# Weight preparation in the opening of a windowed-attention and Mish feed-forward kernel: the engine that scales, rounds and subtracts, and the place of one weight operation

## The chip, the cores and the metric

One Trainium2 chip, of which the kernel uses one core. The metric is the time on the device in microseconds, lower is better. A core has five engines that run their own instruction queues in order and wait for each other on semaphores: TensorE (PE in the rows, its weight loads PEld), VectorE (DVE), ScalarE (ACT), GpSimd (POOL) and SyncE (SP), which here only issues transfers.

## The reference

```
scores = q @ k.T / sqrt(64)              # 8 sequences x 8 heads, 576 positions, head size 64
mask   = (rel >= 0) & (rel < 64)         # each query sees itself and the 63 keys before it
attn   = softmax(scores, masked)
x      = (attn @ v)                      # put together to 4608 tokens x 512
h      = x @ w_in                        # 512 -> 2048
g      = h * tanh(softplus(h))           # Mish
out    = g @ w_out                       # 2048 -> 512
```

The two weight matrices come as 64-bit floating-point numbers, all else in 32 bits.

## The kernel before

**Products in three parts.** Each feed-forward product is made of a high and a low part in a 32-bit format that TensorE reads in one pass: high times high, high times low, low times high. The high part is a rounded copy (xh, gh, wh), the low part the difference to it (xl, gl, wl). So each value needs a rounding copy and a subtraction.

**Weight pieces.** w_in and w_out are loaded in pieces of 128 x 512 numbers of 64 bits into a buffer st (three of them in turn), and every piece is made into 32-bit numbers there. st is seen as pairs of 32-bit words, lo and hi; an operation on one of them steps over every second word. For a piece the generator `stream` (lines 480 to 493) does in turn: the scale of hi by a power of two (`w_scale`), a shift of lo and a clamp of hi (`w_ready`, two TENSOR_SCALAR rows on st), two joins of hi into lo (`w_joined`, two SCALAR_TENSOR_TENSOR rows on st), the round to wh (`w_round`, a CAST row wi<-st or wo_h<-st) and the subtraction to wl (`w_rest`, a TENSOR_TENSOR row wi<-st,wi or wo_l<-st,wo_h), after which the next load into the freed buffer is issued on SP (`w_load`). The next piece's scale is called between the joins of the piece ahead of it. After two pieces of w_in (tile wi) they alternate between w_out (tiles wo_h, wo_l) and w_in. Shift, clamp, joins and subtraction are VectorE's; who scales and rounds is looked up in the table `by`, which the opening changes as it goes. `some(n)` (line 684) takes n steps of the generator; a step is one of shift, clamp, first join, second join, subtraction.

**The opening.** The first 768 tokens (two chunks of 384) are brought through attention in eight units, a unit being one chunk and one pair of heads. A hand-written software pipeline (lines 743 to 809) works on several units at once: iteration u makes the values of unit u - 2 (TensorE, o_ps), the softmax of unit u (VectorE's masks with the row maximum, pr<-s_ps,masks; ScalarE's exponentials; then sm by GpSimd, a reciprocal by VectorE, and pr<-pr,sm by GpSimd), the transposes of unit u - 1 (t_ps on TensorE) and their copies pT (half by ScalarE, half by VectorE), and the parts of x of unit u - 2: xh by ScalarE (`rest_high`), xl by VectorE (`rest_low`). Between these it takes as many weight steps as the table OPS says.

```
    OPS = (0,2,2,2,3,2,2,2,4,3)
```

Every engine runs these instructions in the order of the code, so the place of a line is its place in the engine's queue. In iteration u the order on VectorE is masks of unit u + 1, xl of unit u - 2, the OPS[u] weight steps, the copy pT of unit u - 1, the reciprocal of unit u. Iterations 7 to 9 are written out; the first feed-forward products (h_ps) begin in iteration 6, part by part.

In the first iteration the table `by` is set to ScalarE for the scale and GpSimd for the round; in iteration 7 the round goes back to ScalarE (line 784). After the loop the steps of both chunks follow, a feed-forward slice of 128 at a time, first h_ps and Mish, two slices later the output products (acc), with five weight steps to each; there VectorE, ScalarE and TensorE work on as in the opening, GpSimd builds thinner masks (`thin_masks`, six copies) and is otherwise free until about 104 us.

Of the kernel before, what the change touches and what calls it, by code (L numbers as in the profile page):

```python
# [11 lines left out]
F32 = mybir.dt.float32  # L12
# [4 lines left out]
ALU = mybir.AluOpType  # L17
# [3 lines left out]
OFFSET = 2.0 ** -112  # L21
# [9 lines left out]
def tile_window_attn_mish_ffn(  # L31
# [57 lines left out]
    vec, act, pool, load = (InTurn(e) for e in (nc.vector, nc.scalar, nc.gpsimd, nc.sync))  # L89
# [54 lines left out]
    def acc_bank(t, name):  # L144
        return ps_acc.tile([P, CH], F32, name=name, tag=f"acc{t}")

    def h_bank(name, width=CH):
        return ps_h.tile([P, width], F32, name=name, tag="h_ps")
# [5 lines left out]
    def at_bank(name, width=CH):  # L154
        at_last[0] = next(at_turn)
        return ps_at.tile([P, width], F32, name=name, tag=f"at{at_last[0]}")

    def at_set(n, name):
        return ps_at.tile([P, DO], F32, name=name, tag=f"at{n}")
# [211 lines left out]
    def function(h_ps):  # L371
        shape = list(h_ps.shape)
        t = mp.tile(shape, F32, name="t", tag="t", bufs=TS)
        gh = mp.tile(shape, F32R, name="gh", bufs=GHS)
        gl = mp.tile(shape, F32R, name="gl", bufs=GLS)

        with tc.high_priority(offset=SOON):
            act.activation(t, h_ps, AF.Mish)
            act.activation(gh, h_ps, AF.Mish)
            if held[0]:  # L380
                residues.append((gl, t, gh))
            else:
                pool.tensor_tensor(gl, t, gh.bitcast(F32), ALU.subtract)
        return gh, gl
# [3 lines left out]
    def residue():  # L388
        while residues:
            gl, t, gh = residues.pop(0)  # L390
            vec.tensor_tensor(gl, t, gh.bitcast(F32), ALU.subtract)
# [48 lines left out]
    def w_load():  # L440
        if pieces:
            fn, f = pieces.pop(0)
            loaded.append(fn(f))
# [25 lines left out]

    def w_rest(piece):  # L470
        lo, hi, wh, wl = piece
        vec.tensor_tensor(wl, lo.bitcast(F32), wh.bitcast(F32), ALU.subtract)
        w_load()
        yield

# [4 lines left out]
    def stream():  # L480

        for piece in w_scale(by["scale"]):
            yield from w_ready(piece)
            while piece:
                joined = w_joined(piece)
                yield next(joined)
                ahead = next(w_scale(by["scale"]), None)
                yield next(joined)
                w_round()
                if ahead:  # L490
                    yield from w_ready(ahead)
                yield from w_rest(piece)
                piece = ahead

    def scaled_by(engine):
        return lambda out, in_: engine.tensor_scalar(out, in_, OFFSET, None, ALU.mult)

    rounding = []
    by = {"scale": scaled_by(vec), "round": act.copy}

    slow = []

# [116 lines left out]
    def products_of(u):  # L619
        a, p = units[u]  # L620
        if u == 0:
            banks = [b for t in range(NM) for b in ([at_bank("s_ps"), at_bank("s_ps")], [acc_bank(0, "s_ps"), acc_bank(1, "s_ps")],
                                                     [h_bank("s_ps"), h_bank("s_ps")])[t]]
        elif u % 2 == 0:
            banks = [acc_bank(t, "s_ps") for t in range(2)]
        else:
            banks = [at_set(i, "s_ps") for i in range(2)]
        a.products(p, banks)
        if u + 3 < U:
            a.load(p + 3, "qk")  # L630
        if u + 2 >= U:
            a.load(p + 2, "qk")

    def values_of(u):
        a, p = units[u]
        o_ps = at_set(0, "o_ps")[:, :CH] if u == U - 1 else acc_bank(2, "o_ps")
        outs[u] = o_ps
        with in_order():
            value_products(a.v[p], a.pT.pop(p), [o_ps[:, n:n + BLK] for n in range(0, CH, BLK)])
        if u + 3 < U:  # L640
            a.load(p + 3, "v")

    def rest_high(u):
        a, p = units[u]
        xh, xl = a.new_x()
        act.copy(xh[:, p, :], outs[u])

    def rest_low(u):
        a, p = units[u]
        xh, xl = a.new_x()  # L650
        vec.tensor_tensor(xl[:, p, :], outs.pop(u), xh[:, p, :].bitcast(F32), ALU.subtract)

    def first_half(n):
        c, f = steps[n]
        with in_order():
            return ffn_in(c, atts[c].x, f)

    def step(n, h_ps=None):
        pend.append((*steps[n], function(h_ps or first_half(n))))
# [14 lines left out]
    u = 0  # L674

    OPS = (0,2,2,2,3,2,2,2,4,3)
# [7 lines left out]
    def some(n):  # L684
        for _ in range(n):
            next(ops)

    def summed(u):
        a, p = units[u]
        for _ in normal_parts(u):  # L690
            pass

    def transposed(u):
        a, p = units[u]
        a.te_transpose(p, [acc_bank(h, "t_ps") if u >= U - 2 else h_bank("t_ps") for h in range(2)])

    def copied(u):
        units[u][0].te_copies(units[u][1], (act.copy, vec.tensor_copy))

    def masks(u, squares_=BY_HEAD):  # L700
        a, p = units[u]
        a.masked(p, squares_, exps=False)

    def exps(u, squares_=BY_HEAD):
        a, p = units[u]
        exp(a.pr[p], squares_)
# [11 lines left out]
    def first_parts(u, i):  # L718
        for n, k in PARTS[u][i]:
            first_part(n, k)  # L720
# [22 lines left out]
    for u in range(1, U - 1):  # L743
        if u == 1:
            masks(1)
            summed(0)
            by.update(scale=lambda out, in_: act.mul(out, in_, OFFSET), round=pool.tensor_copy)
        else:
            values_of(u - 2)
        if u > 2:  # L750
            summed(u - 1)
        masks(u + 1)
        cut = 6 if u == 2 else 3
        exps(u, BY_HEAD[:cut])
        if u > 1:
            rest_high(u - 2)
        exps(u, BY_HEAD[cut:])
        if u == 1:
            summed(u)
        if 1 < u < U - 2:  # L760
            products_of(u + 2)
        if u > 1:
            rest_low(u - 2)
        some(OPS[u])
        first_parts(u, 0)
        transposed(u - 1)
        copied(u - 1)
        if u == 1:
            products_of(3)
        first_parts(u, 1)  # L770

    u = U - 1
# [8 lines left out]
    copied(u - 1)  # L781
    act.preload_act_table_set("mish")
    summed(u)
    by.update(round=act.copy)
    some(OPS[u])
    first_parts(u, 1)

    u = U
# [10 lines left out]
    u = U + 1  # L799
# [7 lines left out]
    first_parts(u, 1)  # L807
    residue()
    step(2, early[2])

    ahead = 6
    begin = starts[2] + 4
# [524 lines left out]
```

## Time and profile before

| what | value |
|---|---|
| time, median of 3 runs | 876.74 us (876.33 to 878.66) |
| time of the profiled execution | 876.86 us |
| its span, first to last instruction | 875.1 us |
| TensorE busy | 863.1 us (99%) |
| VectorE, ScalarE, GpSimd busy | 445.4, 457.3, 298.9 us |
| granted TensorE clock | 0.999 of full speed |
| share of the chain that ended last | TensorE 97%, VectorE 1%, ScalarE 1%, transfers 1% |

A row of a timeline gives the start in us from the span's start, the duration, engine and line, the operation, out<-in by the names of the tiles, sizes, how many equal instructions follow each other, and in brackets the engine's idle time before it and who ended it. Nearly all instructions of the opening bear line 83, that of a helper that records them; they are told apart by their tiles. Rows of the chain give start, length and engine with the tile; there an instruction's length reaches to the next of the chain.

### The profile page before, as it was taken

The numbers are of one execution on the slowest core, as the hardware profiler recorded it, in microseconds if no ns is written. First come the engines' busy times: TensorE is split into PE (matmuls) and PEld (weight loads), VectorE is DVE, ScalarE is ACT, GpSimd is POOL, SyncE is SP. The second block draws the span as 40 slices with busy tenths as digits, with TensorE's granted clock in tenths as the row PEclk, the third lists the DMA queues.
The fourth block names the chain that finished last, engine by engine and source line by source line (L and its number), as shares of the span: only waits on it lengthen the run. The fifth ranks groups of instructions, "written<-read, shape, count | busy, mean of one in ns | idle before, by whom it ended". The sixth has DMA issues, their size and how long they took to land.

```text
span 875.1 us, 18918 instructions
## 1 busy us (share of the span) xinstructions
PE 863.1 (99%) x7162; PEld 769.5 (88%) x7162; DVE 445.4 (51%) x1258; ACT 457.3 (52%) x1200; POOL 298.9 (34%) x348
## 2 busy tenths in 40 slices
PE   7899999999999999999999999999999999999998
PEld 6798989888888889988888988899889889989896
DVE  6897979457266676342653442545433525322221
ACT  6865665356555666364655463755643635322322
POOL 3500000168656673342243233342333332222311
PEclk9999999999999999999999999999999999999999
DMA  9544454475766685565565655754754542533402
GB/s 304 177 169 155 136 161 142 148 236 197 243 195 226 205 276 187 183 191 179 162 196 159 219 164 165 229 168 152 239 177 138 159 150 90 199 121 116 137 1 73
DMA packets 83755, 151.52 MB, mean 173 GB/s; under 512 B 9008, under 2 KB 59248, under 8 KB 79568
## 3 DMA queue, kind: packets, MB, share of 16 engines
q1 hardware_dynamic: 62224, 64.74, 23.8%
q10 hardware_dynamic: 13968, 65.87, 23.1%
q0 software_dynamic: 7472, 19.70, 6.8%
q8 instruction: 57, 0.93, 0.4%
q14 instruction: 34, 0.28, 0.1%
HBM read 114.36 MB, written 24.12 MB: 158 GB/s over the span
## 4 chain that ended last, share of the span: by engine, by line
PE 97%; DVE 1%; ACT 1%; DMA 1%; POOL 0%; issue 0%; ACTq 0%
PE acc L133 46%; PE m_ps L133 27%; PE h_ps L133 15%; PE s_ps L133 3%; PE at L133 3%; PE o_ps L133 2%; DMA k_t<-kT 1%; DVE st L83 0%; PE t_ps L341 0%; ACT xh L83 0%; DVE xl L83 0%; DVE pT L83 0%; POOL pr L83 0%; DVE pr L83 0%; DVE wi L83 0%
## 5 line engine op out<-in xcount | busy, mean ns | idle before, releaser
L1052 POOL TENSOR_TENSOR gl<-t,gh 128x384 fp32r<-128x384 f32 x128 | 130.5, 1020 | 321.2 <-ACT gh L1051 121.5
L133 PE MATMUL acc<-wo_h,gh 128*128 128x512 f32 x576 | 227.3, 399 | 0.0
L133 PE MATMUL acc<-wo_l,gh 128*128 128x512 f32 x576 | 226.2, 393 | 0.0
L133 PE MATMUL acc<-wo_h,gl 128*128 128x512 f32 x576 | 223.1, 391 | 0.0
L133 PE MATMUL m_ps<-wi 128*128 128x384 f32 x1152 | 217.4, 337 | 0.0
L133 PEld LDWEIGHTS m_ps<-wi 128*128 128x128 f32 x1152 | 204.2, 188 | 8.2 <-ACT gh L83 0.2
L133 PE MATMUL h_ps<-xh,wi 128*128 128x384 f32 x512 | 141.1, 338 | 0.0
L133 PEld LDWEIGHTS acc<-wo_h,gl 128*128 128x128 f32 x576 | 108.2, 188 | 24.6
L133 PEld LDWEIGHTS acc<-wo_h,gh 128*128 128x128 f32 x576 | 108.0, 188 | 19.4
L133 PEld LDWEIGHTS acc<-wo_l,gh 128*128 128x128 f32 x576 | 108.4, 188 | 15.4
L83 ACT ACTIVATE pr<-pr,mx 128x96 f32<-128x96 f32 (+1 forms) x288 | 105.7, 371 | 15.6 <-DVE mx L83 15.4
L1047 ACT ACTIVATE gh<-t 128x384 fp32r<-128x384 f32 x96 | 50.4, 525 | 117.8 <-DVE t L1064 79.8
L1064 DVE TENSOR_TENSOR u<-u,m_ps 128x384 f32<-128x384 f32 x64 | 35.3, 551 | 142.2 <-PE m_ps L133 141.6
L1064 DVE TENSOR_TENSOR t<-u,m_ps 128x384 f32<-128x384 f32 x96 | 53.1, 553 | 98.7 <-PE m_ps L133 88.8
L133 PEld LDWEIGHTS h_ps<-xh,wi 128*128 128x128 f32 x512 | 93.5, 188 | 2.6
L133 PE MATMUL h_ps<-xl,wi 128*128 128x384 f32 x256 | 86.2, 337 | 0.0
L83 DVE CUSTOM_DVE_ANT_0 pr<-s_ps,masks 128x96 f32<-128x96 f32 (+1 forms) x264 | 51.1, 258 | 53.8 <-PE s_ps L133 53.8
L83 ACT ACTIVATE t<-h_ps 128x384 f32<-128x384 f32 x64 | 31.4, 491 | 61.7 <-PE h_ps L133 56.7
L1048 ACT ACTIVATE t<-t 128x384 f32<-128x384 f32 x96 | 50.5, 526 | 8.5 <-ACT gh L1047 0.4
L83 ACT ACTIVATION_READ_ACCUMULATOR pr<-pr,mx 128x1 f32 x288 | 54.8, 190 | 0.0
L133 PEld LDWEIGHTS h_ps<-xl,wi 128*128 128x128 f32 x256 | 48.1, 188 | 2.3
L83 ACT ACT_TABLE_LOAD x35 | 44.9, 1283 | 7.3 <-DVE mx L83 3.8
(80 smaller groups left out, 963.0 us busy)
## 6 DMA issues: line engine op xcount, KB each, us to landing
wi<-sums ACTq DMA_DIRECT2D x32, 1024.0 KB, 5.5
wi<-sums ACTq DMA_DIRECT2D x32, 768.0 KB, 4.5
v_t<-vN SPq DMA_DIRECT2D x16, 768.0 KB, 6.6
st<-w_in SPq DMA_DIRECT2D x16, 512.0 KB, 3.5
st<-w_out SPq DMA_DIRECT2D x16, 512.0 KB, 3.6
k_t<-kT SPq DMA_DIRECT2D x16, 416.0 KB, 6.6
q_t<-qT SPq DMA_DIRECT2D x16, 384.0 KB, 5.6
pT<-tr SPq DMA_DIRECT2D x118, 48.0 KB, 4.7
```

Of the source, the lines that this page charges most:

```text
L83: i = call(*args, **kw)
L133: i = nc.tensor.matmul(*args, **kw)
L1047: nc.scalar.activation(gh, t, AF.Mish)
L1048: nc.scalar.activation(t, t, AF.Mish)
L1052: nc.gpsimd.tensor_tensor(gl, t, gh.bitcast(F32), ALU.subtract)
L1064: nc.vector.tensor_tensor(out_, a, b, ALU.add)
```

## The change

```diff
     def w_rest(piece):
         lo, hi, wh, wl = piece
-        vec.tensor_tensor(wl, lo.bitcast(F32), wh.bitcast(F32), ALU.subtract)
+        by["rest"].tensor_tensor(wl, lo.bitcast(F32), wh.bitcast(F32), ALU.subtract)
         w_load()
         yield
...
-    by = {"scale": scaled_by(vec), "round": act.copy}
+    by = {"scale": scaled_by(vec), "round": act.copy, "rest": pool}
...
         if u == 1:
             masks(1)
             summed(0)
-            by.update(scale=lambda out, in_: act.mul(out, in_, OFFSET), round=pool.tensor_copy)
+            by.update(scale=scaled_by(pool), round=pool.tensor_copy, rest=pool)
...
             products_of(u + 2)
+        some(OPS[u] - OPS[u] // 2)
         if u > 1:
             rest_low(u - 2)
-        some(OPS[u])
+        some(OPS[u] // 2)
         first_parts(u, 0)
...
     summed(u)
-    by.update(round=act.copy)
     some(OPS[u])
     first_parts(u, 1)
...
     residue()
     step(2, early[2])
+    by.update(scale=lambda out, in_: act.mul(out, in_, OFFSET), round=act.copy, rest=vec)
```

In the loop the weight steps of an iteration are split: the larger half stands in front of xl, the rest behind it. From iteration 1 to 9 GpSimd does the scales, the rounds and the subtractions; after the opening the table is set to ScalarE, ScalarE and VectorE.

On GpSimd, in the softmax of units 3 to 6 (sm and pr are those of the softmax, wi<-st,wi the subtraction and st<-st the scale of a weight piece):

```order
 L83 TENSOR_SCALAR sm<-sm 128x6
 L83 TENSOR_TENSOR pr<-pr,sm 128x768
+L83 TENSOR_TENSOR wi<-st,wi 128x512
+L83 TENSOR_SCALAR st<-st 128x512
 L83 TENSOR_SCALAR sm<-sm 128x6
 L83 TENSOR_TENSOR pr<-pr,sm 128x768
```

Behind the pr of unit 3 the subtraction of the first piece and the scale of the third now stand in front of the sm of unit 4. Two scales stand likewise between the pr of unit 1 and the sm of unit 2, and a subtraction between the pr of unit 5 and the sm of unit 6.

On GpSimd, at the end of the opening, from the softmax of the last unit on (masks is the first of the copies for the thinner masks):

```order
 L83 TENSOR_SCALAR sm<-sm 128x6
 L83 TENSOR_TENSOR pr<-pr,sm 128x768
+L83 TENSOR_SCALAR st<-st 128x512
+L83 CAST wo_h<-st 128x512
+L83 TENSOR_TENSOR wo_l<-st,wo_h 128x512
+L83 TENSOR_SCALAR st<-st 128x512
+L83 CAST wi<-st 128x512
+L83 TENSOR_TENSOR wi<-st,wi 128x512
 L83 COPY masks<-masks 32x3x32 x6
```

Scale, round and subtraction of two pieces now follow the last pr, ahead of the mask copies.

On VectorE, around the low part xl of unit 2, with the first piece's subtraction and the second piece's joins:

```order
 L83 ISA mx 128x1
+L83 SCALAR_TENSOR_TENSOR st<-st 128x512
 L83 TENSOR_TENSOR xl_309<-o_ps,xh_308 128x384
-L83 TENSOR_TENSOR wi<-st,wi 128x512
-L83 SCALAR_TENSOR_TENSOR st<-st 128x512 x2
+L83 SCALAR_TENSOR_TENSOR st<-st 128x512
 L83 COPY pT<-t_ps 128x3x4x32
```

The first join moved ahead of xl and the subtraction is gone from between xl and the copy pT. ScalarE's queue loses five scales and two rounds in the opening. TensorE's and SP's queues stay as they were, but for the first output products, where two matmuls with wo_h now stand ahead of the first with wo_l.

## Rows read from the trace of the kernel before

**Rows 1.** The page, part 1: busy us, share of the span, instructions.
```profile
PE 863.1 (99%) x7162; PEld 769.5 (88%) x7162; DVE 445.4 (51%) x1258; ACT 457.3 (52%) x1200; POOL 298.9 (34%) x348
```

**Rows 2.** Windows: us, busy time of PE, PEld, DVE, ACT, POOL, clock, DMA.
```profile
20.00:35.00 15.00, 11.41 (x190) 8.91 (x181) 12.98 (x58) 13.25 (x58) 8.63 (x11) 1.00 0.88 259
...
45.00:150.00 105.00, 105.00 (x702) 94.20 (x701) 90.41 (x219) 66.59 (x153) 1.48 (x2) 1.00 0.48 155
```

**Rows 3.** The chain that ended last, 23 to 33 us: start, us, what.
```profile
23.28 0.56 DVE xl L83
23.84 0.60 DVE wi L83
24.43 0.61 DVE st L83
...
25.77 0.47 DVE pT L83
...
31.72 0.60 DVE wi L83
32.32 0.60 DVE st L83
32.92 0.48 DVE pT L83
```

**Rows 4.** Timeline of VectorE, 11 to 48 us.
```profile
11.35 2.00 DVE L83 TENSOR_SCALAR st<-st 128x512 uint32<-128x512 uint32 x2
...
31.16 0.56 DVE L83 TENSOR_TENSOR xl<-o_ps,xh 128x384 fp32r<-128x384 f32 x1 [0.19 <-ACT xh L83]
...
40.61 0.75 DVE L83 TENSOR_TENSOR wo_l<-st,wo_h 128x512 fp32r<-128x512 f32 x1
...
43.08 0.55 DVE L83 TENSOR_TENSOR xl<-o_ps,xh 128x384 fp32r<-128x384 f32 x1
43.55 0.75 DVE L83 TENSOR_SCALAR st<-st 128x512 uint32<-128x512 uint32 x2
...
47.75 0.68 DVE L83 TENSOR_TENSOR wo_l<-st,wo_h 128x512 fp32r<-128x512 f32 x1
```

**Rows 5.** Timeline of GpSimd, 11 to 39 us.
```profile
11.52 1.54 POOL L83 TENSOR_TENSOR pr<-pr,sm 128x768 f32<-128x768 f32 x1 [0.31 <-DVE sm L83]
...
21.94 1.47 POOL L83 TENSOR_TENSOR pr<-pr,sm 128x768 f32<-128x768 f32 x1 [0.54 <-DVE sm L83]
24.56 0.56 POOL L83 TENSOR_SCALAR sm<-sm 128x6 f32<-128x6 f32 x1 [1.15 <-ACT pr L83]
...
29.90 1.47 POOL L83 TENSOR_TENSOR pr<-pr,sm 128x768 f32<-128x768 f32 x1 [0.62 <-DVE sm L83]
...
36.20 0.23 POOL L83 TENSOR_SCALAR sm<-sm 128x6 f32<-128x6 f32 x1 [1.09 <-ACT pr L83]
36.88 1.75 POOL L83 TENSOR_TENSOR pr<-pr,sm 128x768 f32<-128x768 f32 x1 [0.45 <-DVE sm L83]
```

**Rows 6.** Tile w, 150 to 330 us: count, ns least/median/most, first and last start.
```profile
L853 DVE TENSOR_TENSOR w<-w x32: 419/426/1753, 165.4 to 310.5; 128x256 f32<-128x256 f32 x32
```

**Rows 7.** Groups, 9 to 46 us, of ScalarE and of VectorE: count | busy us, mean ns | idle before.
```profile
L83 ACT ACTIVATE st<-st 128x512 f32<-128x512 f32 x6 | 4.1, 683 | 0.0
...
L83 DVE TENSOR_TENSOR xl<-o_ps,xh 128x384 fp32r<-128x384 f32 x8 | 4.5, 557 | 3.2 <-ACT xh L83 3.2
```

**Rows 8.** Groups of GpSimd over the whole span.
```profile
L1052 POOL TENSOR_TENSOR gl<-t,gh 128x384 fp32r<-128x384 f32 x128 | 130.5, 1020 | 321.2 <-ACT gh L1051 121.5 <-PE acc L133 94.3 <-ACT t L1048 76.7
...
L857 POOL TENSOR_TENSOR w<-w,high 128x1024 fp32r<-128x1024 f32 x8 | 19.3, 2412 | 61.2 <-DVE high L855 61.2
...
L83 POOL CAST wi<-st 128x512 fp32r<-128x512 f32 x2 | 1.3, 674 | 0.0
```

**Rows 9.** Timeline of TensorE, from 19 us.
```profile
19.48 0.89 PE L133 MATMUL s_ps<-k_t,q_t 64*64 64x128 f32 x24 [0.15 <-DMA k_t<-kT]
```

**Rows 10.** Timeline of TensorE, 43 to 50 us.
```profile
43.81 0.33 PE L133 MATMUL h_ps<-xl,wi 128*128 128x384 f32 x1
...
49.01 0.39 PE L133 MATMUL acc<-wo_l,gh 128*128 128x512 f32 x1
```

## The prediction

> **What bounds the kernel now.** I read the page's busy times, then the windows by stage, then the chain that ended last, and last the engines' timelines in the opening. TensorE is busy 863.1 of 875.1 us [rows 1]. In the windows the idle time lies in the opening: from 20 to 35 us TensorE works 11.41 of 15.00 us, from 45 to 150 us all 105.00 [rows 2]. So nothing that the change does elsewhere than before about 45 us can gain anything, and whatever makes TensorE late there shifts the rest of the span by the same amount, unless a slack takes it up. That caps the subject: all that the change touches lasts some 35 us.
>
> In that stretch the chain runs through VectorE: the low part xl, the weight operations, the copy pT, then TensorE's values o_ps, ScalarE's xh and the next xl [rows 3]. The weight operations therefore lie in the chain: the subtraction wi takes 0.60 us of it at 23.84 and again at 31.72, each joining operation st 0.60 to 0.70. VectorE's only idle time per round is the 0.19 us ahead of xl [rows 4]. This is what the edit aims at.
>
> **The port that VectorE and GpSimd share.** Before costing anything one must see what the two engines do to each other. At 11.35 two TENSOR_SCALAR of VectorE took 2.00 us, the same pair at 43.55 0.75 [rows 4]; beside the first ran GpSimd's pr from 11.52 to 13.06 [rows 5], and the pair ended 0.29 after it. At 24.56 GpSimd's sm took 0.56 us instead of 0.23, while a join ran on VectorE [rows 3, 5], and pr at 36.88 took 1.75 instead of 1.47 for the same reason [rows 5]. In the later stage 32 equal additions w<-w, two inputs from SBUF, take 419 ns at least and up to 1753 [rows 6]. So these kinds exclude each other: the second waits for nearly the whole of the first and then ends its own length less about 0.13 us later. xl, which has one of its two inputs in PSUM, took 557 ns in the mean of eight [rows 7], some of them beside a pr, and shows no such thing. All that moves to GpSimd here reads SBUF, and VectorE's remaining weight operations are of the excluded kinds.
>
> **Prices.** Seven operations leave ScalarE (five scales st, a round wo_h and a round wi) and four subtractions leave VectorE; GpSimd gets all eleven. ScalarE's row gives 683 ns for a scale [rows 7]; what ScalarE loses is no gain by itself, since it stands in the chain only with xh. On GpSimd a round of the same size, reading the same alternate words, is a row: 674 ns [rows 8]. The subtraction: the same form takes 1020 ns at 384 columns and 2412 at 1024 [rows 8], so 1.02 + 128 x 1.39/640 = 1.30; the means hold some blocking, and I take 1.27 us. Bounds: 1.06 (the slope of pr, 1.47 us for 768 columns [rows 5] against 0.23 for sm's six) and 1.37 (1.02 x 512/384). No row shows GpSimd scale 512 columns. It has one input, as the round has, but writes alternate words: 0.67 (the round) to 1.27 (a subtraction); I take 0.75, next to the round.
>
> [...]
>
> **The sum, in the order of time.**
> Iterations 1 and 2: a scale now waits behind pr(1), so the clamp that needs it ends near 13.9 instead of 13.35 and some 0.8 us arise. At 19.48 TensorE waits for k_t to land anyway [rows 9], and I cost this at nothing; without that landing it would be up to 0.8.
> Iterations 4 and 5: pr(3) ends at 23.41 [rows 5]. The join now in front of xl waits for it and ends near 23.95; GpSimd's subtraction, next in its queue, waits for that join and ends near 25.1; xl and the second join follow, the latter near 25.6; pT comes about where it did (25.77 [rows 3], 0.1 earlier). So here the saved 0.60 us is spent on waiting. Behind the subtraction stands the scale, to 26.25, and behind that sm, which before started at 24.56 [rows 5]: the reciprocal is 0.35 late. VectorE gets the 0.19 ahead of xl back. Left: **0.2 us**.
> Iteration 6: before, xl, subtraction 0.60, join 0.60, pT at 32.92 [rows 3]. Now the subtraction starts on GpSimd when pr ends (29.90 + 1.47 = 31.37 [rows 5]) and ends at 32.64; the join waits, and pT follows 0.5 us behind, at 33.15: **0.25 us**.
> End of the opening: pr(7) ends at 38.63 [rows 5], 39.1 with the above. Behind it GpSimd has scale, round and subtraction twice, 2 x (0.75 + 0.67 + 1.27) = 5.4 us without a gap, and VectorE's joins and clamps fall between them. Before, from 40.61 the subtraction, two joins and a gl brought xl at 43.08 [rows 4]. Now the first join waits for GpSimd's subtraction (to 42.15, join to 42.7), the second for the next scale (to 43.3, join to 43.9), gl 0.47: xl starts at 44.3, 1.2 late. TensorE used this xl at 43.81 [rows 10], 0.18 after its end at 43.63. So TensorE is 1.0 late, of which 0.45 was there: **0.5 us**.
> Behind it: the pair of TENSOR_SCALAR at 43.55 falls on the second subtraction and the joins on the six mask copies, which now stand behind the weights. VectorE's queue slips by some 2.1 us, so wo_l, before at 47.75 to 48.43 [rows 4], ends at 50.5. Its matmul was at 49.01 [rows 10], 0.58 later; 2.1 - 0.58 - 1.0 = **0.5 us** more. The weight loads on SP, issued when a buffer's subtraction is done, go out about 1 us later, and VectorE's queue, 2.1 us late, asks for them later by more; from there on work and orders are those of before.
> Sum 0.2 + 0.25 + 0.5 + 0.5 = 1.45, say 1.5 us. If scale and subtraction turn out otherwise, the scale counts about 3.5 times in it, the subtraction 4 times (so many of them have a waiter behind them). Low ends: 1.5 - 3.5 x 0.08 - 4 x 0.21 = 0.4; high ends: 1.5 + 3.5 x 0.52 + 4 x 0.10 = 3.7. The profiled execution took 876.86 us, 0.12 above the median 876.74; 876.86 + 1.45 = **878.3 us**, 0.2% over the median. I count 0.3% (2.6 us) as what a measurement can tell from no change: 874.1 and 879.4.
>
> **Rivals.**
> The relief wins: the collisions fall otherwise than I lay them, or cost little. Then VectorE's chain loses 0.60 twice and 0.67 once, and gains the 0.19 of several rounds, while reciprocals waiting behind the longer GpSimd queue give back some 0.5: 1.4 us gained, 875.5. For it: the chain [rows 3]. Against: the blocked instructions [rows 4 to 6]. It decides if joins find the port free at 24.4, 31.8 and 41.3.
> The slow scale: GpSimd scales at the rate at which it subtracts, 1.27 us. Then sm at 24.56 and the queue after 38.6 carry 3.5 times the difference: 1.5 + 3.5 x 0.52 = 3.3 us, 3.7 with the subtraction at its upper bound: 880.2 to 880.6. It passes 879.4 from a scale of about 1.05. For it: writing alternate words, which no row shows; against it: one input, as the round has. [...]
> Slack takes it up: landings such as that of k_t at 19.48, or a weight needed later than I think, swallow the delays: 876.9. That the order would not be what the text of the change says is excluded by the built program's order.
>
> **Chances.** Forecast 0.47 (877.5 to 879.2), relief 0.2, slow scale 0.2, slack 0.13. Slower by over 0.3%: the larger part of the slow scale and a tail of the forecast, 0.23. Faster by over 0.3% lies beyond the whole relief: 0.05. Within: 0.72. The range from 875.4 to 880.4 holds most of the relief and a part of the slow scale.
>
> **What would show it.** Right: subtractions on GpSimd near 1.27 and scales near 0.75 alone, joins of VectorE at 1.2 to 1.7 us around 24, 32 and 41; a wait of TensorE of about 0.5 us near 44 on xl and one near 50 on wo_l; TensorE's first full stretch 1.5 us later, and the rest of the trace merely shifted. Wrong: joins at 0.69 throughout, pT of iteration 6 before 32.9, or TensorE without a wait at 44; or a scale over 1 us.

## The result, and the profile after

| | before | after |
|---|---|---|
| median | 876.80 us (6 runs, 876.24 to 878.66) | 881.35 us (6 runs, 880.41 to 882.92) |
| ratio, 95% interval | | 1.0051 [1.0038, 1.0065] |
| profiled execution | 876.86 us, span 875.1 | 880.41 us, span 878.6 |

The change makes the kernel 4.55 us (0.5%) slower. I had forecast 878.3 us and a range to 880.4. A second set of five runs on another chip gave 881.71 against 876.97, ratio 1.0051 [1.0039, 1.0064].

The page and the windows of the kernel after, to be read beside [rows 1, 2] (the clock is the last column but two):

```profile
PE 863.5 (98%) x7162; PEld 769.1 (88%) x7162; DVE 446.0 (51%) x1254; ACT 453.1 (52%) x1193; POOL 315.9 (36%) x359
```

```profile
20.00:35.00 15.00, 11.11 (x172) 8.92 (x164) 12.87 (x56) 11.70 (x52) 12.50 (x13) 0.89 0.75 226
...
45.00:150.00 105.00, 103.54 (x691) 92.03 (x690) 90.91 (x217) 64.47 (x149) 7.53 (x11) 1.00 0.48 153
```

TensorE does the same work; what is new is idle time before 53 us, and a stretch from 31.0 to 34.4 us with a granted clock of 0.50 (the clock records of the two profiles hold 1.00 and 0.50 alone), called the half clock below. GpSimd is busy 12.50 of the 15 us from 20 to 35, where it was 8.63 [rows 2]. Its groups, 9 to 52 us (count | busy us, mean ns | idle before):

```profile
L83 POOL TENSOR_SCALAR st<-st 128x512 f32<-128x512 f32 x5 | 8.9, 1779 | 0.5 <-DMA st<-w_in 0.5
L83 POOL TENSOR_TENSOR wi<-st,wi 128x512 fp32r<-128x512 f32 x3 | 4.4, 1477 | 0.1
```

A scale takes GpSimd 1.78 us in the mean. I had taken 0.75, with 1.27 as the upper bound [rows 8]. GpSimd's timeline tells what of it is the operation itself and what is waiting for VectorE (the prediction's port, a name for these waits; what the two engines share is not shown):

```profile
12.98 1.55 POOL L83 TENSOR_SCALAR st<-st 128x512 f32<-128x512 f32 x1
15.08 1.57 POOL L83 TENSOR_SCALAR st<-st 128x512 f32<-128x512 f32 x1 [0.54 <-DMA st<-w_in]
...
23.70 1.75 POOL L83 TENSOR_TENSOR wi<-st,wi 128x512 fp32r<-128x512 f32 x1
25.41 2.01 POOL L83 TENSOR_SCALAR st<-st 128x512 f32<-128x512 f32 x1
27.50 0.24 POOL L83 TENSOR_SCALAR sm<-sm 128x6 f32<-128x6 f32 x1
28.11 1.47 POOL L83 TENSOR_TENSOR pr<-pr,sm 128x768 f32<-128x768 f32 x1 [0.37 <-DVE sm L83]
...
32.81 1.30 POOL L83 TENSOR_TENSOR wi<-st,wi 128x512 fp32r<-128x512 f32 x1
...
40.33 1.76 POOL L83 TENSOR_SCALAR st<-st 128x512 f32<-128x512 f32 x1
42.04 0.66 POOL L83 CAST wo_h<-st 128x512 fp32r<-128x512 f32 x1
42.78 1.37 POOL L83 TENSOR_TENSOR wo_l<-st,wo_h 128x512 fp32r<-128x512 f32 x1
44.12 2.00 POOL L83 TENSOR_SCALAR st<-st 128x512 f32<-128x512 f32 x1
```

Alone the scale takes 1.55 to 1.57, behind an operation of VectorE up to 2.01. The subtraction is where I put it (1.30 alone at 32.81, forecast 1.27), the round too (0.66, forecast 0.67). The sm that [rows 5] show at 24.56 now starts at 27.50. VectorE's timeline:

```profile
14.57 0.43 DVE L83 TENSOR_SCALAR st<-st 128x512 f32<-128x512 f32 x1 [2.88 <-POOL st L83]
...
23.34 0.95 DVE L83 SCALAR_TENSOR_TENSOR st<-st 128x512 uint32<-128x512 uint32 x1
...
24.68 1.32 DVE L83 SCALAR_TENSOR_TENSOR st<-st 128x512 uint32<-128x512 uint32 x1
...
27.77 0.19 DVE L83 RECIPROCAL sm<-sm 128x6 f32<-128x6 f32 x1 [1.31 <-POOL sm L83]
...
43.02 2.73 DVE L83 SCALAR_TENSOR_TENSOR st<-st 128x512 uint32<-128x512 uint32 x2
46.14 0.55 DVE L83 TENSOR_TENSOR xl<-o_ps,xh 128x384 fp32r<-128x384 f32 x1
...
51.69 0.67 DVE L83 TENSOR_TENSOR wo_l<-st,wo_h 128x512 fp32r<-128x512 f32 x1
```

There are two new waits of VectorE for GpSimd: 2.88 us of the clamp for the first scale, and 1.31 us of a reciprocal for the sm behind the third scale. The joins are drawn out as forecast (two in 2.73 us at 43.02); xl is ready 3.06 us later than in [rows 4] (46.14 for 43.08), wo_l 3.94. TensorE, its rows with a wait:

```profile
15.52 0.91 PE L133 MATMUL o_ps<-pT,v_t 128*64 128x64 f32 x22 [1.31 <-DVE pT L83]
...
29.64 0.87 PE L341 MATMUL t_ps<-ident,pr 128*128 128x128 f32 x6 [1.39 <-POOL pr L83]
...
46.74 0.44 PE L133 MATMUL h_ps<-xl,wi 128*128 128x384 f32 x1 [1.26 <-DVE xl L83]
52.41 0.51 PE L133 MATMUL acc<-wo_l,gh 128*128 128x512 f32 x1 [0.20 <-DVE wo_l L83]
```

The two matmuls of [rows 10], at 43.81 and 49.01 before, are 2.93 and 3.40 us late, and from 55 us on all is shifted by 3.5 to 3.6. What follows is read by this shift: the start of a matmul less the start of the same one in the profile before.

| profile | at 8.4 us | 14.8 | 23.8 | 28.0 | 43.8 | 54.7 |
|---|---|---|---|---|---|---|
| after | -0.05 | +1.17 | +0.33 | +1.63 | +2.93 | +3.60 |
| scale_back | +0.92 | +0.92 | +0.13 | +0.04 | -0.05 | +0.54 |
| scale_first | -1.05 | +0.60 | +0.55 | +0.45 | +0.37 | +0.98 |
| scale_early | -0.63 | +1.04 | +1.21 | +2.51 | +2.39 | +2.96 |
| fill_5 | -0.10 | +0.93 | +1.28 | +2.59 | +3.90 | +4.53 |
| place_again | +0.56 | +0.43 | -0.59 | -0.72 | -0.81 | -0.81 |
| place_more | -0.86 | -0.69 | -0.74 | +0.38 | +0.59 | +0.60 |
| scale_only | +0.36 | +1.51 | +1.27 | +2.48 | +3.16 | +3.26 |
| scale_one | -0.17 | +1.05 | +0.21 | +0.12 | +0.01 | +0.59 |
| scale_late | -0.32 | -0.35 | -0.98 | -1.08 | +0.28 | +0.90 |

The first column lies ahead of everything that the change touches, and spans 2 us: so far do single executions differ by the landings of the first transfers (ahead of 8 us TensorE waits for k_t 0.58 and 0.39 us in the kernel before, 0.25 and 0.67 in the kernel after). Therefore verdicts go by medians of several runs, and a profile tells where steps arise. Distances below are medians less the median of the kernel before, taken beside it on the same chip (876.29 to 876.98).

### The profile page after: what moved, and what is told of

It reads as the page before. It is cut to its first block, busy times and chain, and to the rows that moved or that the text cites. A ratio compares the mean times of both kernels' runs of the same rounds, so it can differ in the third digit from the quotient of the medians.

```text
span 878.6 us, 18919 instructions
## 1 busy us (share of the span) xinstructions
PE 863.5 (98%) x7162; PEld 769.1 (88%) x7162; DVE 446.0 (51%) x1254; ACT 453.1 (52%) x1193; POOL 315.9 (36%) x359
## 4 chain that ended last, share of the span: by engine, by line
PE 94%; DVE 3%; POOL 2%; DMA 1%; issue 0%; ACTq 0%; ACT 0%; POOLq 0%
PE acc L133 46%; PE m_ps L133 27%; PE h_ps L133 15%; PE at L133 3%; PE s_ps L133 3%; DVE st L83 1%; PE o_ps L133 1%; POOL pr L83 1%; POOL st L83 1%; DVE pr L83 1%; DMA k_t<-kT 1%; DVE pT L83 0%; PE t_ps L341 0%; DVE xl L83 0%; POOL wi L83 0%
## 5 line engine op out<-in xcount | busy, mean ns | idle before, releaser
L133 PEld LDWEIGHTS acc<-wo_h,gh 128*128 128x128 f32 x576 | 107.9, 187 | 19.4
```

The lines of the kernel that those rows point to most:

```text
L133: i = nc.tensor.matmul(*args, **kw)
```

## The experiments

Theory A: the GpSimd scale, at twice the price taken, makes the loss. Theory B: the port does, that is the waits of GpSimd and VectorE for each other, whatever the scale costs. Others: the place of the weight steps, TensorE's clock. The diffs below leave out the lines that set an entry of the table ahead of the loop and back behind iteration 9.

**The parts, one by one.** scale_back: the changed kernel with

```diff
-            by.update(scale=scaled_by(pool), round=pool.tensor_copy, rest=pool)
+            by.update(scale=lambda out, in_: act.mul(out, in_, OFFSET), round=pool.tensor_copy, rest=pool)
```

> The changed kernel with its scales back on ScalarE; place and GpSimd's rounds and subtractions stay. Theory A (GpSimd's scale of 1.55 us, against the 0.75 I had taken, makes the loss): about 0.4 us over the kernel before, 877.0 to 877.6. Theory B (the port: subtractions on GpSimd and VectorE's joins wait for each other, whatever the scale costs): most of the loss stays, 879.5 to 881. In the trace under A, VectorE's clamp at 14.6 no longer waits, sm of unit 4 starts near 25.5 instead of 27.5, and xl is ready near 43.6.

Measured 876.27 us (11 runs), -0.7 against the kernel before, ratio 0.9990 [0.9981, 0.9999]. Without its scales the change is no loss, even a small gain; A's number was too high, since it knew nothing of the gain of the place (below). B falls: the subtractions still meet the joins (a join at 24.48 takes 1.32 us there too), yet the time is not lost. In the timeline of VectorE shift and clamp end at 14.3 and xl starts at 43.12, 0.04 after [rows 4]:

```profile
12.27 2.00 DVE L83 TENSOR_SCALAR st<-st 128x512 uint32<-128x512 uint32 x2
...
24.48 1.32 DVE L83 SCALAR_TENSOR_TENSOR st<-st 128x512 uint32<-128x512 uint32 x1
...
43.12 0.55 DVE L83 TENSOR_TENSOR xl<-o_ps,xh 128x384 fp32r<-128x384 f32 x1
```

scale_only: the kernel before, and only the scales of iterations 1 to 9 on GpSimd.

```diff
-            by.update(scale=lambda out, in_: act.mul(out, in_, OFFSET), round=pool.tensor_copy)
+            by.update(scale=scaled_by(pool), round=pool.tensor_copy)
...
```

> The kernel before with nothing but its scales of iterations 1 to 9 on GpSimd (rounds, subtractions and places as before). Theory A: 3 to 4 us over the kernel before (2.4 of them by iteration 6, 1.4 at the end of the opening), 879.8 to 880.8. Theory B: under 1.5 us, 877 to 878.3, since the port is then used by four subtractions less. A third theory (the half clock of TensorE near 31 to 34 us is a cost of its own): A's sum plus 0.5 to 1 us, and the half clock is to be seen in the windows here too.

Measured 879.94 us, +3.0, ratio 1.0038 [1.0026, 1.0051]: A's range. But part of it comes by way of TensorE's clock, as the third theory had it. The clock was 0.50 from 28.0 to 31.4 us, behind a wait of TensorE of 1.29 us for a late pT; TensorE's score products and VectorE's next copy pT there:

```profile
28.99 1.56 PE L133 MATMUL s_ps<-k_t,q_t 64*64 64x128 f32 x24
```

```profile
31.81 0.56 DVE L83 COPY pT<-t_ps 128x384 f32<-128x384 f32 x1 [0.97 <-PE t_ps L341]
```

The products take 1.56 us where they took 0.89 in the kernel before, VectorE then waits 0.97 us for TensorE's transposes, and the shift grows there from 1.43 to 2.72 us.

rest_only: the kernel before, and only the subtractions of the opening on GpSimd.

```diff
-        vec.tensor_tensor(wl, lo.bitcast(F32), wh.bitcast(F32), ALU.subtract)
+        by["rest"].tensor_tensor(wl, lo.bitcast(F32), wh.bitcast(F32), ALU.subtract)
...
```

> The kernel before with nothing but its subtractions of the opening on GpSimd. Theory A: 0.5 us over the kernel before (0.2 in iteration 4, 0.3 in iteration 6), 877.0 to 877.7, joins at 1.2 to 1.7 us behind a subtraction. Theory B: 2 to 3 us over it. If the port cost nothing it would be 1.4 us faster, 875.4.

Measured 877.49 us, +0.5, ratio 1.0010 [1.0001, 1.0019]. The collisions eat what VectorE saves and half a microsecond more, near what my sum had (0.2 and 0.25 in iterations 4 to 6; in the profile the shift grows by 0.19 and 0.25 there).

place_only: the kernel before, and only the place.

```diff
+        some(OPS[u] - OPS[u] // 2)
         if u > 1:
             rest_low(u - 2)
-        some(OPS[u])
+        some(OPS[u] // 2)
```

> The kernel before with the weight steps split around xl and nothing else. Theory A: no change, 876.6 to 877.0 (modelled -0.1 us). A theory that the place costs (xl late by a join of 0.6 us in iterations 4 to 6, and TensorE's first parts with it): 0.6 us or more over the kernel before.

Measured 875.84 us (11 runs), -1.1, ratio 0.9986 [0.9977, 0.9995]. That was expected by nobody, so it ran again:

> The kernel before with the weight steps split around xl, a second time, since the first came out 1.1 us below the kernel before where my working had given nothing. If the gain is real: 875.2 to 876.0 where the kernel before takes 876.3 to 877.0, a ratio under 1 with its whole interval. If it was chance of the transfers before 19 us: within 0.5 us of the kernel before.

Measured 875.82 us (11 runs), -1.1, ratio 0.9988 [0.9979, 0.9997]. The gain is real, and this version beats both kernels. VectorE's xl of iteration 2 in the kernel before, and its timeline in place_only:

```profile
16.01 0.56 DVE L83 TENSOR_TENSOR xl<-o_ps,xh 128x384 fp32r<-128x384 f32 x1 [0.63 <-ACT xh L83]
```

```profile
14.69 0.69 DVE L83 SCALAR_TENSOR_TENSOR st<-st 128x512 uint32<-128x512 uint32 x1
15.42 0.56 DVE L83 TENSOR_TENSOR xl<-o_ps,xh 128x384 fp32r<-128x384 f32 x1
...
22.17 0.95 DVE L83 TENSOR_TENSOR wi<-st,wi 128x512 fp32r<-128x512 f32 x1
...
23.66 0.54 DVE L83 TENSOR_TENSOR xl<-o_ps,xh 128x384 fp32r<-128x384 f32 x1
...
29.80 1.01 DVE L83 TENSOR_TENSOR wi<-st,wi 128x512 fp32r<-128x512 f32 x1
30.74 0.55 DVE L83 TENSOR_TENSOR xl<-o_ps,xh 128x384 fp32r<-128x384 f32 x1
```

VectorE works through: no xl of iterations 2 to 6 waits any more, where before there were waits for xh of 0.63 us in iteration 2 and of 0.19 in the next four [rows 4 show one], 1.39 us in all; 0.6 us go back, since the two subtractions now fall on pr (0.95 and 1.01 us instead of 0.68). That leaves 0.8 of the 1.1 us. Does more work ahead of xl give more?

```diff
+        ahead_of_low = OPS[u] if u < 6 else OPS[u] - OPS[u] // 2
+        some(ahead_of_low)
         if u > 1:
             rest_low(u - 2)
-        some(OPS[u])
+        some(OPS[u] - ahead_of_low)
```

> The kernel before with all weight steps of iterations 2 to 5 ahead of xl, and those of iteration 6 split. If VectorE's idle time ahead of xl (0.63 us in iteration 2, 0.19 in the others) is all that the place gives back: as place_only, 875.5 to 876.2. If a later xl holds up the bank o_ps, and with it the next values: 0.3 to 0.6 us over the kernel before, 877.3.

Measured 877.55 us, +0.8, ratio 1.0006 [0.9997, 1.0014]. No: the gain of place_only is gone. VectorE's rows of iterations 4 and 5:

```profile
24.48 0.55 DVE L83 TENSOR_TENSOR xl<-o_ps,xh 128x384 fp32r<-128x384 f32 x1
...
29.64 0.56 DVE L83 COPY pT<-t_ps 128x384 f32<-128x384 f32 x1 [0.89 <-PE t_ps L341]
```

With all the steps ahead of it xl is late (24.48 for 23.28 before), but TensorE's shift is -0.74 us at 23.8 and still at 26.3. The loss arises behind that, up to +0.61 at 29.5: TensorE has waited 1.51 us, its clock is 0.50 from 25.7 to 29.1 us, and VectorE waits for its transposes. So in this execution it was the half clock that took the gain; whether it does in the others is not shown.

**Which scales.** scale_early is the changed kernel with the last two scales back on ScalarE, scale_late with only those two on GpSimd:

```diff
     act.preload_act_table_set("mish")
     summed(u)
+    by.update(scale=lambda out, in_: act.mul(out, in_, OFFSET))
     some(OPS[u])
```

(scale_late: `scale=scaled_by(pool)` in this place, ScalarE's scale in iteration 1.)

> The changed kernel, its scales on GpSimd only up to iteration 6 (three of them), the last two back on ScalarE. Theory A in its parts: the early three cost 2.0 us over scale_back (one in front of sm of unit 4, the clamp of iteration 1), so 2.4 us over the kernel before by the prices 1.55 and 1.30, 878.2 to 879.2. If the scales cost only by the crowding of GpSimd behind the last softmax, nothing is left: 876.3.

> The changed kernel, its scales on ScalarE up to iteration 6, and only the last two on GpSimd. Theory A: the two stand in a row of scale, round and subtraction of twice 3.5 us behind the last softmax, xl near 45.5, 2.4 us over scale_back, 878.3 to 879.3. If the early ones make the loss, it is 876.3.

Measured 879.82 (+3.5, [1.0027, 1.0051]) and 878.13 us (+1.8, [1.0014, 1.0031]). Both groups cost, the early three above their forecast, the late two a little below theirs; over scale_back the two groups cost 4.2 and 2.6 us by themselves, and 5.3 together. scale_first and scale_one leave two and one of the early scales on GpSimd, in the changed kernel:

```diff
+        if u == 4:
+            by.update(scale=lambda out, in_: act.mul(out, in_, OFFSET))
         some(OPS[u] - OPS[u] // 2)
```

(scale_one: `u == 2`.)

> The changed kernel, with only its first two scales (iterations 1 and 2) on GpSimd and the other three on ScalarE. My prediction costed these two at nothing, since TensorE waits for k_t near 19.5 us anyway: then it is scale_back's time, some 0.7 us below the kernel before, 875.6 to 876.5. Without that cover, by the price 1.55, the clamp of iteration 1 is 1.6 us late: 0.8 to 1.6 us over scale_back, 877.0 to 878.0. With scale_early, the difference is the third scale alone, ahead of sm of unit 4: 2 to 3.5 us.

> The changed kernel with only its first scale (iteration 1) on GpSimd, the other four on ScalarE. If the first scale makes the loss of scale_first, since VectorE's clamp waits for it: 0.8 to 1.6 us over scale_back by the price of 1.55, 877.0 to 877.9, and with the further 1.5 us of most executions of scale_first up to 879.4. If the second one does, waiting on GpSimd for the piece to land: scale_back's time, 876.0 to 876.6.

Measured 879.37 (+2.4, [1.0012, 1.0034]) and 878.69 us (+1.7, [1.0009, 1.0026]). scale_first lies above both its forecasts, scale_one in the wider of its ranges. So the row of steps, each distance to the kernel before, is scale_back -0.7, with the first scale +1.7, the second +2.4, the third +3.5, the last two +4.6. By the medians the first scale alone is worth 2.4 us, more than any other; VectorE's timeline of scale_one names its waiter:

```profile
14.46 0.43 DVE L83 TENSOR_SCALAR st<-st 128x512 f32<-128x512 f32 x1 [2.89 <-POOL st L83]
```

Behind this clamp stands the copy pT for which TensorE's o_ps waits. The profiles show about half of the 2.4 us: up to iteration 6 scale_one and scale_late differ in this scale alone, their profiles start alike (-0.17 and -0.32 at 8.4 us), and scale_one is 1.40 us later at 14.8 and 1.20 at 28.0. The rest lies between medians and is not placed; the profiled scale_one was the second fastest of eleven.

The eleven times of scale_first lie in two groups, four from 877.78 to 878.08 and seven from 879.33 to 880.41. I profiled it once more:

> The same kernel as scale_first, one profile more: of its eleven times four lay near 877.9 and seven near 879.6 us, and the first profile (878.08) was one of the four. If the second scale's wait for its weight piece to land, with sm of unit 2 queued behind it, makes the difference, an execution near 879.6 shows that sm later than 17.0 us by 1 us or more. If TensorE's clock does, the half clock lasts longer there.

It gave 877.95, of the lower group again: there sm of unit 2 starts at 17.83, 0.8 us later than in the first profile, and the time is the same, which speaks against that sm as the cause. No execution of the upper group was profiled. The changed kernel was profiled again, too:

> The changed kernel again: 880.5 to 882.5, ratio near 1.005. Its first profile was the fastest of six times, and in it the delay of 1.2 us at 14.8 us was gone by 19.5 since the full clock came at 13.9 us. If that was chance and not the cover by k_t on which I built, most executions, and this profile, keep the delay through 20 us.

Median 881.71 us, but the profiled execution was 880.72, and its shifts repeat the first profile's (+1.26 at 14.8 us, +0.42 at 23.8). That refutes neither reading. What can be compared are the 24 score products behind the late o_ps. In the kernel before and in the kernel after:

```profile
15.38 1.56 PE L133 MATMUL s_ps<-k_t,q_t 64*64 64x128 f32 x24
```

```profile
16.36 0.89 PE L133 MATMUL s_ps<-k_t,q_t 64*64 64x128 f32 x24
```

In scale_early, whose shift at 23.8 us is 0.9 larger than that of the changed kernel:

```profile
15.06 1.54 PE L133 MATMUL o_ps<-pT,v_t 128*64 128x64 f32 x22 [1.71 <-DVE pT L83]
16.53 1.56 PE L133 MATMUL s_ps<-k_t,q_t 64*64 64x128 f32 x24
```

Both profiles of the changed kernel did them in 0.89 us, scale_early in 1.56, at half clock: the granted clock was 0.50 from 11.8 to 18.6 us. fill and fill_5 below show the same (0.50 until 19.2 and 19.4; shifts +1.32 and +1.28 at 23.8). So with TensorE idle behind the late clamp, the full clock comes at 14 us in some executions, and at 18 to 20 in others, which lose about 0.9 us more. Between them lie the two profiles of scale_first, full clock from 17.7 and 15.7 us and shifts of +0.55 and +0.48, both of its lower group. Without early GpSimd scales the full clock came by 16.9 (in the kernel before the six transposes take 1.54 us at 10.95 and 0.87 at 16.87), but for shift_only below, which had the half clock from 19.6 to 23.0. This fits the two groups and medians that lie above the profiled executions; since no execution of an upper group was profiled, it is argued, not shown.

**The half clock at 31 us.** The profile after has the clock at 0.50 from 31.0 to 34.4 us, behind TensorE's waits of 1.04 and 1.39 us; the profile before has none there. fill and fill_5 put matmuls without use into these waits; their results are overwritten. fill_5:

```diff
...
+        if u == 4:
+            with in_order():
+                for _ in range(5):
+                    pe(banks[0][:, :P], ident, ident, start=True, stop=True)
         a.te_transpose(p, banks)
```

(fill has six there, and five into the bank o_ps ahead of the values of unit 3.)

> The changed kernel with eleven further matmuls of the identity into banks that the next instructions overwrite, five ahead of the values of unit 3 and six ahead of the transposes of unit 4, where TensorE stood idle for 1.0 and 1.4 us. If the half clock from 31.0 to 34.4 us follows from that idleness and costs by itself: full clock from 14 us to the end and 0.5 to 1.2 us less than the changed kernel (880.2 to 880.9). If the clock costs nothing there, since the other engines set the pace: full clock and the same 881.4, or, where the added matmuls hold up the values, up to 0.5 us more.

> The changed kernel with five matmuls of the identity ahead of the transposes of unit 4 only, which take some 1.35 us of TensorE where it stood idle for 1.39 us. If the half clock at 31 us follows from the idle TensorE and has a price: no half clock, and 0.3 to 0.8 us below the changed kernel, 880.5 to 881.0. If the other engines set the pace there: no half clock and 881.2 to 881.6. If the half clock stays all the same, the idle time ahead of the transposes is not what brings it.

Measured 883.53 (+7.2) and 883.58 us (+6.7), 2.1 to 2.7 us more than the changed kernel's distance: neither theory's number. The windows from 31.0 to 34.4, of the kernel after and of fill:

```profile
31.00:34.40 3.40, 3.17 (x31) 2.85 (x30) 2.58 (x16) 2.54 (x14) 2.72 (x2) 0.50 0.29 95
```

```profile
31.00:34.40 3.40, 2.24 (x33) 1.72 (x32) 3.21 (x18) 2.89 (x13) 2.69 (x4) 1.00 0.57 190
```

The half clock is gone in both (1.00 over this window), where both profiles of the changed kernel have it (0.50 and 0.54), so there the idle TensorE does bring it. But the stretch from 28.0 to 43.8 us loses 1.30 us in the kernel after (+1.63 to +2.93), 1.34 in fill (+2.63 to +3.97) and 1.31 in fill_5: the half clock costs nothing there, GpSimd and VectorE set the pace, and in all three TensorE waits 1.2 to 1.3 us for xl at the end of the stretch. That holds for this stretch alone; in scale_only and place_more, above, VectorE waited for a TensorE at half clock. The time that both fills lose arises elsewhere: about 1 us ahead of 28 us (the late full clock above), and 1.5 to 2.4 us between 250 and 350 us, in part one idle time of TensorE with nothing to wait for (1.6 and 1.4 us, "issue" in its waits). The cause of the latter stays open.

**The price of the scale.** probe: the kernel before with GpSimd instructions on a tile of its own, behind the mask copies; odd and even are the tile's alternate words, left and right its halves.

```diff
             thin_masks(pool)
+            probe(pool)
...
+        for out_, in_ in ((odd, odd), (left, left), (left, even), (odd, right), (odd[:, :half // 2], odd[:, :half // 2])):
+            for _ in range(3):
+                engine.tensor_scalar(out_, in_, OFFSET, None, ALU.mult)
+        for out_, in_ in ((odd, odd), (left, left), (left, even)):
+            for _ in range(3):
+                engine.tensor_copy(out_, in_)
+        for out_, x, y in ((left, left, right), (odd, odd, odd)):
+            for _ in range(3):
+                engine.tensor_tensor(out_, x, y, ALU.subtract)
```

> The kernel before with rows of GpSimd instructions on a tile of its own behind the mask copies, three of each: TENSOR_SCALAR of 384 columns on alternate words in place, on contiguous words, from alternate to contiguous, from contiguous to alternate, of 192 columns on alternate words; COPY of 384 on alternate words in place, on contiguous, from alternate to contiguous; TENSOR_TENSOR of 384 contiguous and on alternate words. If the writing of alternate words makes the scale slow: about 1.2 us for 384 columns where it writes them, 0.5 where it doesn't, COPY likewise. If TENSOR_SCALAR as such is slow: 1.2 us in all four, COPY 0.5 in all three. The shortest of each three is taken, the longer ones wait for VectorE. No time for the whole is forecast but that of the kernel before to 1 us, since GpSimd has no other work there.

By tile and window, ns least/median/most of three each: TENSOR_SCALAR on alternate words in place and on contiguous ones, COPY on alternate and on contiguous ones, TENSOR_TENSOR on contiguous and on alternate ones:

```profile
L83 POOL TENSOR_SCALAR probe<-probe x3: 1271/1353/1403, 41.1 to 44.0; 128x384 f32<-128x384 f32 x3
L83 POOL TENSOR_SCALAR probe<-probe x3: 1217/1269/1553, 45.4 to 48.3; 128x384 f32<-128x384 f32 x3
...
L83 POOL COPY probe<-probe x3: 540/742/882, 61.3 to 62.9; 128x384 f32<-128x384 f32 x3
L83 POOL COPY probe<-probe x3: 583/591/845, 63.7 to 65.0; 128x384 f32<-128x384 f32 x3
L83 POOL TENSOR_TENSOR probe<-probe x3: 1079/1080/1343, 68.6 to 70.9; 128x384 f32<-128x384 f32 x3
L83 POOL TENSOR_TENSOR probe<-probe x3: 1022/1156/1157, 72.3 to 74.8; 128x384 f32<-128x384 f32 x3
```

The kind sets the price, not the step: TENSOR_SCALAR 1.22 to 1.27 us for 384 columns whichever words it takes, TENSOR_TENSOR with its two inputs 1.02 to 1.08, COPY 0.54 to 0.58. What I did not forecast: the whole took 887.93 us. GpSimd worked from 41.1 to 75.8 without a gap, and TensorE then waited 2.9 us for VectorE's gl and 0.9 for its wo_l, +11.1 us by 100 us. About half of that arises in one stretch at half clock, behind TensorE's waits, in which it was busy for 9.10 of 10.30 us (TensorE's is the first busy time, the clock the last column but two):

```profile
75.80:86.10 10.30, 9.10 (x66) 6.75 (x65) 9.70 (x29) 3.04 (x6) 0.00 (x0) 0.50 0.46 150
```

A GpSimd that works "in its free time" was not free here, beside a VectorE that in the kernel before is busy 31.66 of the 35.00 us from 41 to 76.

If the kind is dear, a product would be cheaper. scale_tt:

```diff
+    offset = const.tile([P, 1], F32, name="offset")
+    vec.memset(offset, OFFSET)
+
+    def product(out, in_):
+        pool.tensor_tensor(out, in_, offset.to_broadcast([P, WP]), ALU.mult)
...
-            by.update(scale=scaled_by(pool), round=pool.tensor_copy, rest=pool)
+            by.update(scale=product, round=pool.tensor_copy, rest=pool)
```

> The changed kernel, its scale on GpSimd written as TENSOR_TENSOR, a product with one number spread over the columns. If TENSOR_SCALAR as a kind is the dear one: 1.1 to 1.3 us for a scale alone, and 1.0 to 1.8 us (four times the 0.25 to 0.45 saved) less than the changed kernel, 879.5 to 880.3. If any arithmetic on alternate words takes 1.5 us: no change, 881.4. A product with two reads from SBUF may also meet VectorE's port more, which would take some of the gain.

Measured 886.49 us, +9.6: no theory's number. The scale itself took 1.04 us at the least, as foreseen, but the matmuls with 512 columns had become a little longer up to the end (those of the low parts 394 ns in the mean from 350 to 850 us, 391 to 392 before). scale_tt_pad widens the tile (`[P, 32]`, its first column used):

> scale_tt with the number's tile widened from 4 to 128 bytes a partition, so that the tiles behind it begin where an even address does. In scale_tt every matmul behind the opening took some 0.8% longer, 6.5 us of its 9.6. If that came of the shifted tiles: it is gone, and 879.5 to 881.5 is left, the true effect of a TENSOR_TENSOR scale. If not: 886 again.

Measured 886.53 us: no help. shift_only takes the product away and leaves the tile, in the kernel before:

```diff
+    offset = const.tile([P, 32], F32, name="offset")
+    vec.memset(offset, OFFSET)
```

> The kernel before with nothing but one more tile of 128 bytes a partition, filled once and not used. Behind it every tile of the other pools begins 128 bytes later. If this is what made all matmuls behind the opening 0.8% longer in scale_tt and scale_tt_pad: some 6 us over the kernel before, 882 to 883.5. If it came of the product itself: the time of the kernel before, 876.5 to 877.3.

Measured 883.39 us, +6.6, ratio 1.0067 [1.0052, 1.0083]: the tile alone does it. That it does so by where it puts all tiles behind it is inferred, since the one memset is all else that it adds. Groups of TensorE from 350 to 850 us, before and shift_only:

```profile
L133 PE MATMUL m_ps<-wi 128*128 128x384 f32 x1077 | 203.1, 336 | 0.0
...
L133 PE MATMUL acc<-wo_h,gl 128*128 128x512 f32 x359 | 140.4, 391 | 0.0
```

```profile
L133 PE MATMUL m_ps<-wi 128*128 128x384 f32 x1078 | 203.4, 336 | 0.0
...
L133 PE MATMUL acc<-wo_h,gl 128*128 128x512 f32 x354 | 139.8, 395 | 0.0
```

So not every matmul is longer: the m_ps, with 384 columns, keep their 336 ns. Less that, the product leaves 9.6 - 6.6 = 3.0 us of loss, where the scale as TENSOR_SCALAR has 4.6: some 1.6 us back, within the 1.0 to 1.8 expected, if the two effects add up. The profiles don't bear it out: at 60 us, ahead of most of the longer matmuls, scale_tt and scale_tt_pad are 3.3 and 3.2 us late, the two of the changed kernel 3.6 and 3.7, though with a full clock from 14 us where theirs came at 18.9 and 19.8. What the product gives back is not shown.

## Why the prediction was wrong

By its own steps:

- **The price of the scale: wrong.** "It has one input, as the round has" was the choice that failed. I took 0.75 us next to the round, bounds 0.67 to 1.27; alone it measured 1.55. The rival "slow scale" had the right mechanism and named its point (above 1.05 us slower than 0.3%), but its 1.27, the price of a subtraction, was too low as well: on GpSimd this one-input operation is dearer than the two-input one (1.55 against 1.30 us). The probe's steps of 8 and 4 bytes cost alike (1.27 and 1.22 us for 384 columns): not the step makes this operation dear here. With 1.55 in place of 0.75 and the 3.5 that I gave as its weight, the sum is 1.45 + 3.5 x 0.80 = 4.25, and 881.1 us. The total would have been right, but by luck: it has nothing for the first two scales, the dearest by the medians, and nothing for what the place gives back.
- **Iterations 1 and 2 at nothing: wrong.** I had 0.8 us there and let the landing of k_t swallow it. [Rows 9] say how much it could: 0.15 us is what TensorE waited, so anything later than that goes through (in other profiles that wait is 0 to 0.84 us). By the medians the first two scales cost 3.1 us (scale_first less scale_back), 2.4 of them by the first one, of which the profiles show 1.2. In the profile after, where the delay did shrink from 1.17 to 0.33 us before 24 us, it was the full clock, there 3 us earlier than in the profile before (13.9 for 16.9), and not k_t that took it up.
- **Iterations 4 and 5, 0.2: mechanism right, too small by the price; iteration 6, 0.25, as forecast.** The subtraction and the joins met as laid out (joins of 1.32 us; rest_only +0.5). But sm, which I had 0.35 late by a scale that ends at 26.25, came at 27.50 behind one that ended at 27.42, and TensorE waited 1.39 us for the pr: the shift grows by 1.30 us from 23.8 to 28.0. In iteration 6 it grows by 0.25, from 1.49 to 1.74. The third scale is worth 1.1 us (scale_early less scale_first).
- **End of the opening and wo_l, 0.5 and 0.5: right places; larger at xl, as forecast at wo_l.** TensorE waits 1.26 us for xl and 0.20 for wo_l, at the two matmuls named; there the shift grows from 1.73 to 2.93 and on to 3.40 us. (In my working the times 42.15 and 43.3 hold 0.36 and 0.40 us beyond the prices, for which no row stands.) The last two scales cost 1.1 us (the change less scale_early) to 2.6 (scale_late less scale_back).
- **The place of the weight steps: missed, and with the other sign.** I gave VectorE "the 0.19 ahead of xl back" and counted nothing for it. [Rows 7] had 3.2 us of xl waiting for xh; filling the 1.39 us of iterations 2 to 6 is worth 1.1 us (place_only, twice). place_only to scale_back is +0.4 for subtractions and rounds.
- The relief rival fell (nothing of the change but its place gains), slack too, on the ground just given. The rest of the trace is merely shifted, as forecast.

The steps from the kernel before to the changed one are -1.1 (place), +0.4 (subtractions and rounds), +2.4, +0.7, +1.1 (first three scales), +1.1 (last two). That they sum to 4.6 is no check, since each is the difference to the step ahead of it, and in another order they differ (the last two scales: 1.1 or 2.6). By the intervals a step between two such distances is uncertain by an estimated 1.1 to 1.6 us. So the place, measured directly and twice, the first scale and the five scales together are shown by the times; the sizes of the smaller steps are not.

## What to carry to other kernels

Price an operation on another engine by the same kind on that engine, not by the number of its inputs (here 0.66 and 1.55 us for two operations with one, 1.30 with two); without a row of the kind, the upper bound has to be open. A wait of 0.15 us covers 0.15 us of lateness, however important the transfer looks that ends it. And before moving work off a chained engine, look for that engine's own waits inside the chain: half of the steps moved ahead of the waiting instruction gave 1.1 us here, with no other engine involved.

## What the runs showed of the hardware

- GpSimd's TENSOR_SCALAR took 1.55 us for 128x512 on alternate words; 1.2 to 1.3 for 128x384, on alternate and on contiguous words alike; 0.72 for 128x192 on alternate ones. TENSOR_TENSOR took 1.30 and 1.02 to 1.08 for 512 and 384 columns, a CAST of 512 columns 0.66.
- An unused tile of 128 bytes a partition made the 128x512 matmuls of the low parts 395 instead of 391 to 392 ns long in the mean, left the 128x384 m_ps at 336, and made the kernel 6.6 us slower, more than the change under study. Two kernels with 4 and 128 bytes lost alike (886.49 and 886.53 us in all); why is open, and that the place of the tiles behind it does it is inferred. An experiment that adds a tile needs its own control.
- What the half clock cost depended on who waited for TensorE. In the changed kernel, from 31.0 to 34.4 us, it cost nothing (1.30 us lost from 28 to 43.8 with it, 1.34 and 1.31 without), since others set the pace. In scale_only and place_more VectorE waited 0.97 and 0.89 us for transposes made at half clock, and in probe TensorE was busy at it for 9.10 of 10.30 us.
